# Two matmul layers after attention: five token blocks instead of six in layer 1, and two slices of h in one PSUM bank at the end of layer 2

## The chip, the cores and the metric

The kernel runs on one core of one Trainium2 chip. The time is device microseconds (us) of one execution; lower is better. TensorE (PE) multiplies, VectorE (DVE), ScalarE (ACT) and GpSimd (POOL) do the element work, SyncE (SP) issues the DMAs.

## The reference

Attention with two sparse masks (local for the first four heads, strided for the last four), then two layers over 2304 tokens, each 512 wide inside 2048 and back:

```python
x = attention(q, k, v)                       # (4*576, 512)
h = np.maximum(x @ w_in, 0.0); x1 = (h * h) @ w_out        # layer 1, w_in 512x2048, w_out 2048x512
h = x1 @ w2_in                                             # layer 2
P = a[0] + a[1]*h + a[2]*h**2 + a[3]*h**3
Q = 1.0 + abs(b[0])*abs(h) + abs(b[1])*h**2
out = (P / (Q + 1e-6)) @ w2_out
```

## The kernel before

**Numbers.** Every operand is split in a high and a low part (`xh`, `xl`; `wh`, `wl`; `gh`, `gl`), and each product is three matmuls: high by high, high by low, low by high.

**Layer 1** goes over token blocks j of `WIDTHS` columns and, in each, over 16 slices f of 128 of the 2048 inner features. `h_unit` (L414 to L420) makes one slice of h: 4 parts of the 512 inputs by 3 matmuls, 12 matmuls whose moving operand is as wide as the block, into one PSUM bank. `act1` (L426) squares and splits it on ACT, DVE and POOL. `o_unit1` (L457 to L465) adds it to four accumulators that stay in PSUM for the block: again 12 matmuls as wide as the block. It runs `LAG` = 2 slices behind. `evac1` (L467) copies the accumulators out, and they go to DRAM.

**Layer 2** goes over blocks of `WIDTHS2`. `unit2` (L664) makes h the same way, `act2` (L602) puts the rational function together (five ACT, two POOL and three DVE operations), `split2` (L633) splits the result on ACT and POOL, and `o_unit2` (L641) adds it to one accumulator per 128 tokens, with 512 columns moving. It runs `LAG2` = 4 slices behind; in blocks of 384 two slices of h come first and then two of the output. The first `EARLY` = 5 slices of layer 2 run between the last five of layer 1, here called the layer change. `load_x1` (L591) brings the next block's input from DRAM and splits it on ACT and POOL.

**Attention** is cut in pieces (`ORDER`, L232): two strided ones per batch, and one local piece per block of layer 1. The first three run ahead of layer 1. The others are spread by `PLAN` (L675): scores with softmax, transposes, and values, each at a named slice (j, f) of layer 1.

**Weights.** In block 0 those of layer 1 are converted (`feed_w`), in blocks 1 to 4 those of layer 2 (`spill_w`, L575): one load, ACT, three DVE and two POOL operations, two stores.

**Order and buffers.** A recording layer puts the instructions on each engine's queue, mostly in the order of the code, and puts in the waits. Buffers turn by tag: `g_tile` (L423) gives "r", "gh" and "gl" to both layers. PSUM has eight banks: seven turn (`psum`), and one (`psum_w`) holds converted weights in block 0 and later one accumulator or one bank of scores (`acc_bank`, L451). SP issues the DMAs in its queue's order.

Of the kernel before, what the change touches and what calls it, by code (L numbers as in the profile page):

```python
# [34 lines left out]
C_L, C_S, C_ID, C_END = 0, 384, 440, 568  # L35
# [85 lines left out]
def moe_kernel(ctx, tc, qs, vs, ql, vl, w1, w2, a, b, masks, eye, out):  # L121
# [650 lines left out]
```

## Time and profile before

| | |
|---|---|
| median of 3 runs | 863.61 us (863.11 to 866.34) |
| profiled execution: its own time, its span | 863.71 us, 861.9 us |
| busy share of the span: PE, DVE, POOL, ACT | 98%, 70%, 61%, 54% |
| layer 1, layer 2 | about 27 to 480 us, 440 to 862 us |

The span is what the profiler saw between the first and the last instruction; 1.8 us lie around it. A busy PE is one that has a matmul under way.

### The profile page before, as it was taken

Reading aid. Unit: us, or ns where it says so; the run is one execution under the profiler, and the core shown is the slowest. Engines: PE = TensorE matmul, PEld = TensorE weight load, DVE = VectorE, ACT = ScalarE, POOL = GpSimd, SP = SyncE. Lnnn points to the kernel's source line nnn. Section 1 sums busy time; section 2 is a strip of 40 time slices with the busy share of each in tenths; the row PEclk is TensorE's granted clock in tenths of the full one; section 3 lists DMA queues with packets and bytes.
Section 4 is the critical chain, followed back from the end, with each engine's and each line's share of the span. In section 5 each row is a group of like instructions: output and inputs, shape, how many; then the busy total and the mean of one; then the engine's idle time right before and its main releaser. Section 6 shows DMA issues by size and latency. Waiting matters only on the chain.

```text
span 861.9 us, 15809 instructions
## 1 busy us (share of the span) xinstructions
PE 848.7 (98%) x6141; PEld 761.3 (88%) x6146; DVE 601.7 (70%) x744; ACT 465.8 (54%) x908; POOL 529.9 (61%) x511
## 2 busy tenths in 40 slices
PE   7999999999999999999999999999999999999998
PEld 4788789999999999999998888999888889888886
DVE  6999947635556555552125788878898888889885
ACT  4555633333433334332246666776776677767663
POOL 2787736535554555563334577877787787867774
PEclk9999999999999999999999999999999999999999
DMA  9982345535554446645764400110010001000001
GB/s 339 366 285 71 105 155 185 195 96 177 155 198 155 137 135 203 203 142 172 269 234 155 144 13 13 45 38 10 9 47 12 14 13 62 1 0 37 1 1 49
DMA packets 38379, 100.04 MB, mean 116 GB/s; under 512 B 4512, under 2 KB 8352, under 8 KB 38304
## 3 DMA queue, kind: packets, MB, share of 16 engines
q1 hardware_dynamic: 38304, 99.03, 34.4%
q8 instruction: 48, 0.79, 0.4%
q14 instruction: 27, 0.22, 0.1%
HBM read 72.80 MB, written 26.21 MB: 115 GB/s over the span
## 4 chain that ended last, share of the span: by engine, by line
PE 91%; ACT 2%; DVE 2%; POOL 2%; DMA 2%; issue 1%; SPq 0%; POOLq 0%; ACTq 0%; DVEq 0%
PE h L420 44%; PE acc L650 22%; PE acc L465 21%; PE ps_vl L360 1%; DMA qkl<-in_ql 1%; DMA wraw<-in_w 1%; PE ps_vs L360 1%; PE ps_sl L299 1%; PE ps_tl L351 0%; POOL p L618 0%; PE ps_ss L299 0%; DVE h L622 0%; PE ps_ts L351 0%; DVE wraw L190 0%; POOL wl L200 0%
## 5 line engine op out<-in xcount | busy, mean ns | idle before, releaser
L420 PE MATMUL h<-xh,wh 128*128 128x384 f32 (+2 forms) x704 | 248.2, 353 | 2.2 <-DVE rq L631 1.3
L420 PE MATMUL h<-xh,wl 128*128 128x384 f32 (+2 forms) x704 | 246.4, 350 | 0.0
L420 PE MATMUL h<-xl,wh 128*128 128x384 f32 (+2 forms) x704 | 246.4, 350 | 0.0
L622 DVE RECIPROCAL h<-w 128x512 f32<-128x512 f32 (+1 forms) x80 | 242.7, 3033 | 1.0 <-POOL w L619 1.0
L618 POOL TENSOR_TENSOR p<-p,hs 128x512 f32<-128x512 f32 (+1 forms) x80 | 94.7, 1183 | 110.3 <-ACT p L616 110.3
L420 PEld LDWEIGHTS h<-xh,wh 128*128 128x128 f32 x704 | 132.4, 188 | 14.5 <-DVE rq L631 1.6
L420 PEld LDWEIGHTS h<-xl,wh 128*128 128x128 f32 x704 | 132.5, 188 | 10.5
L420 PEld LDWEIGHTS h<-xh,wl 128*128 128x128 f32 x704 | 132.3, 188 | 10.0
L465 PE MATMUL acc<-gh,wh 128*128 128x384 f32 (+2 forms) x384 | 128.8, 337 | 0.0
L465 PE MATMUL acc<-gh,wl 128*128 128x384 f32 (+2 forms) x384 | 128.6, 335 | 0.0
L465 PE MATMUL acc<-gl,wh 128*128 128x384 f32 (+2 forms) x384 | 128.6, 335 | 0.0
L443 POOL TENSOR_TENSOR gl<-r,gh 128x384 fp32r<-128x384 f32 (+1 forms) x75 | 74.4, 994 | 72.5 <-ACT gh L442 69.3
L650 PE MATMUL acc<-wh,gl 128*128 128x512 f32 x288 | 112.5, 391 | 0.4 <-POOL gl L638 0.4
L650 PE MATMUL acc<-wl,gh 128*128 128x512 f32 x288 | 112.4, 390 | 0.0
L650 PE MATMUL acc<-wh,gh 128*128 128x512 f32 x288 | 111.9, 389 | 0.0
L439 DVE TENSOR_TENSOR r<-r 128x384 f32<-128x384 f32 (+1 forms) x75 | 47.6, 634 | 88.4 <-ACT r L435 88.3
L613 ACT ACTIVATE sq<-h 128x512 f32<-128x512 f32 (+1 forms) x80 | 44.9, 561 | 115.4 <-PE h L420 111.4
L620 DVE SCALAR_TENSOR_TENSOR p<-p,co,h 128x512 f32<-128x512 f32 (+1 forms) x80 | 54.3, 679 | 67.5 <-POOL p L618 67.0
L638 POOL TENSOR_TENSOR gl<-rq,gh 128x512 fp32r<-128x512 f32 (+1 forms) x80 | 94.6, 1184 | 2.5 <-ACT gh L637 2.5
L619 POOL TENSOR_TENSOR w<-w,sq 128x512 f32<-128x512 f32 (+1 forms) x80 | 94.5, 1181 | 0.0
L435 ACT ACTIVATE r<-h 128x384 f32<-128x384 f32 (+2 forms) x91 | 44.4, 488 | 91.3 <-PE h L420 91.3
L442 ACT CAST gh<-r 128x384 fp32r<-128x384 f32 (+2 forms) x91 | 46.7, 513 | 78.7 <-DVE r L439 77.8
(109 smaller groups left out, 1339.5 us busy)
## 6 DMA issues: line engine op xcount, KB each, us to landing
wraw<-in_w SPq DMA_DIRECT2D x64, 512.0 KB, 4.3
w_scratch<-sph SPq DMA_DIRECT2D x32, 256.0 KB, 3.9
w_scratch<-spl SPq DMA_DIRECT2D x32, 256.0 KB, 3.2
wh<-w_scratch SPq DMA_DIRECT2D x16, 512.0 KB, 3.7
wl<-w_scratch SPq DMA_DIRECT2D x16, 512.0 KB, 4.6
qks<-in_qs SPq DMA_DIRECT2D x8, 585.0 KB, 5.4
out_dram<-osb SPq DMA_DIRECT2D x18, 256.0 KB, 2.1
qkl<-in_ql SPq DMA_DIRECT2D x8, 400.0 KB, 4.0
```

The lines of the kernel that those rows point to most:

```text
L420: nc.tensor.matmul(ps[:, :n], w[:, c], x, start=(kk == 0 and i == 0), stop=(kk == KT - 1 and i == 2))
L439: nc.vector.tensor_tensor(h, h, h, ALU.mult)
L442: last_act = nc.scalar.copy(gh, h).ins
L443: low = lambda: (nc.vector if psum_h or j == 0 else nc.gpsimd).tensor_tensor(gl, h, gh.bitcast(F32), ALU.subtract)
L465: nc.tensor.matmul(acc[j][e][:, : WIDTHS[j]], w[:, c], g, start=(f == 0 and i == 0), stop=(f == NF - 1 and i == 2))
L613: keep(nc.scalar.activation(sq, h, AF.Square))
L618: keep(nc.gpsimd.tensor_tensor(p1, p1, hs, ALU.mult))
L619: keep(nc.gpsimd.tensor_tensor(w, w, sq, ALU.add))
L620: keep(nc.vector.scalar_tensor_tensor(p1, p1, a1, h, ALU.add, ALU.mult))
L622: keep(nc.vector.reciprocal(h, w))
L638: keep(nc.gpsimd.tensor_tensor(gl, rq, gh.bitcast(F32), ALU.subtract))
L650: nc.tensor.matmul(p, g[:, t * P : (t + 1) * P], w[:, c], start=(f == 0 and i == 0), stop=(f == NF - 1 and i == 2))
```

## The change

Layer 1 has five blocks, of 512, 384, 512, 512 and 384 columns, where it had six (512, 256 and four of 384). So there is one local piece of attention fewer, the local pieces are up to 512 wide, and `PLAN` places the pieces in blocks 0 to 3. The layer 2 weights are converted in blocks 1 to 3 (8, 8 and 16 halves), in block 3 one in every slice. Layer 2 has four blocks of 512 and one of 256. In that last block two slices of h stand side by side in one bank, `act2` takes them together as 512 columns, and `o_unit2` adds both: 2 tiles by 2 slices by 3 matmuls. The input's places in SBUF turn in another way, the tag "r" has three buffers instead of four, the staged raw weights two instead of three. In the first five slices of layer 2 `w` and `hs` have places of their own (`whs`), and the next block's input is loaded at slices 6, 8, 10 and 12 there instead of 1, 4, 7 and 10. For the very last slice DVE adds `w` and `sq`, not POOL.

```diff
-WIDTHS = (512, 256, 384, 384, 384, 384)
+WIDTHS = (512, 384, 512, 512, 384)
-WIDTHS2 = (512, 384, 512, 384, 512)
+WIDTHS2 = (512, 512, 512, 512, 256)
+FSTEP = [512 // w for w in WIDTHS2]
-C_L, C_S, C_ID, C_END = 0, 384, 440, 568
+C_L, C_S, C_ID, C_END = 0, 576, 632, 760
...
-            raw = stage.tile([P, DM, 2], I32, tag="wraw", bufs=3, name=f"wraw{layer}_{f}_{part}")
+            raw = stage.tile([P, DM, 2], I32, tag="wraw", bufs=2, name=f"wraw{layer}_{f}_{part}")
...
-    ORDER = [("s", 0, 2), ("s", 0, 3), ("l", 0), ("l", 1), ("s", 1, 2), ("s", 1, 3), ("l", 2), ("l", 3),
-             ("s", 2, 2), ("s", 2, 3), ("l", 4), ("s", 3, 2), ("s", 3, 3), ("l", 5)]
+    ORDER = [("s", 0, 2), ("s", 0, 3), ("l", 0), ("l", 1), ("s", 1, 2), ("s", 1, 3), ("l", 2),
+             ("s", 2, 2), ("s", 2, 3), ("l", 3), ("s", 3, 2), ("s", 3, 3), ("l", 4)]
...
+        if layer and f % FSTEP[j]:
+            ps = ps[:, n:]
...
-        return gpool.tile([P, 512], dtype, tag=tag, name=name, bufs=4 if tag == "r" else 3)[:, :n]
+        return gpool.tile([P, 512], dtype, tag=tag, name=name, bufs=3)[:, :n]
...
-            acc[j] = [acc_bank(f"acc0_{j}_{e}", e == 0 and j % 2 == 1) for e in range(KT)]
+            acc[j] = [acc_bank(f"acc0_{j}_{e}", e == 0 and j in (1, 3, 4)) for e in range(KT)]
...
-        n = WIDTHS2[j]
+        n = 512
...
-        w = g_tile("gh", f"w{j}_{f}", n)
-        hs = g_tile("gl", f"hs{j}_{f}", n)
+        if j == 0 and f < EARLY:
+            pair = xpool.tile([P, 2, n], F32, tag=f"x{'hl'[f % 2]}12", name=f"whs{f}")
+            w, hs = pair[:, 0], pair[:, 1]
+        else:
+            w = g_tile("gh", f"w{j}_{f}", n)
+            hs = g_tile("gl", f"hs{j}_{f}", n)
...
-        keep(nc.gpsimd.tensor_tensor(w, w, sq, ALU.add))
+        last = (j, f) == (NB2 - 1, NF - FSTEP[-1])
+        keep((nc.vector if last else nc.gpsimd).tensor_tensor(w, w, sq, ALU.add))
...
-            for i, (g, w) in enumerate(pairs):
-                nc.tensor.matmul(p, g[:, t * P : (t + 1) * P], w[:, c], start=(f == 0 and i == 0), stop=(f == NF - 1 and i == 2))
+            for d in range(FSTEP[j]):
+                wh, wl = wt[1, f + d]
+                cg = slice(d * WIDTHS2[j] + t * P, d * WIDTHS2[j] + (t + 1) * P)
+                for i, (g, w) in enumerate(((gh, wh), (gh, wl), (gl, wh))):
+                    nc.tensor.matmul(p, g[:, cg], w[:, c], start=(f + d + i == 0), stop=(f + d == NF - 1 and i == 2))
...
-        h_unit(1, j, f, ps)
+        for d in range(FSTEP[j]):
+            h_unit(1, j, f + d, ps)
...
-        if j + 1 < NB2 and f in (1, 4, 7, 10):
-            load_x1(j + 1, f // 3)
+        if j + 1 < NB2 and f in X_AT[j > 0]:
+            load_x1(j + 1, X_AT[j > 0].index(f))
...
+    X_AT = (6, 8, 10, 12), (1, 4, 7, 10)
     PLAN = {
-        3: ((0, 2), (0, 4), (0, 5)), 4: ((0, 6), (0, 8), (0, 9)), 5: ((0, 10), (0, 12), (0, 13)), 6: ((1, 3), (1, 7), (1, 9)),
...
+        3: ((0, 2), (0, 4), (0, 5)), 4: ((0, 6), (0, 8), (0, 9)), 5: ((0, 10), (0, 12), (0, 13)), 6: ((1, 1), (1, 4), (1, 5)),
+        7: ((1, 5), (1, 8), (1, 9)), 8: ((1, 9), (1, 12), (1, 13)), 9: ((1, 13), (2, 4), (2, 5)), 10: ((2, 5), (2, 8), (2, 9)),
+        11: ((2, 9), (2, 12), (2, 13)), 12: ((2, 13), (3, 4), (3, 5)),
...
-    spills = (0, 5, 13, 21, 2 * NF)
+    spills = (0, 8, 16, 2 * NF)
...
-        if WIDTHS2[j] == 384 and f % 2 == 0:
-            continue
```

**At the layer change, POOL's queue.** Before (`p` and `w` with the slice's number are `act2`'s, `gl` is `split2`'s, `xl` is `load_x1`'s for block 1):

```order
L618 TENSOR_TENSOR p_0_5571<-p_0_5571,hs_0_5570 128x512
L619 TENSOR_TENSOR w_0_5569<-w_0_5569,sq_0_5568 128x512
L618 TENSOR_TENSOR p_1_5633<-p_1_5633,hs_1_5632 128x512
L619 TENSOR_TENSOR w_1_5631<-w_1_5631,sq_1_5630 128x512
L598 TENSOR_TENSOR xl_1_5646<-xraw_0_5647,xh_1_5645 128x384
L618 TENSOR_TENSOR p_2_5702<-p_2_5702,hs_2_5701 128x512
L619 TENSOR_TENSOR w_2_5700<-w_2_5700,sq_2_5699 128x512
L638 TENSOR_TENSOR gl_0_0_5715<-rq_0_5572,gh_0_0_5714 128x512
```

The same place of the change:

```order
L624 TENSOR_TENSOR p_0_5002<-p_0_5002,whs_5001 128x512
L626 TENSOR_TENSOR whs_5001<-whs_5001,sq_0_5000 128x512
L624 TENSOR_TENSOR p_1_5063<-p_1_5063,whs_5062 128x512
L626 TENSOR_TENSOR whs_5062<-whs_5062,sq_1_5061 128x512
L624 TENSOR_TENSOR p_2_5125<-p_2_5125,whs_5124 128x512
L626 TENSOR_TENSOR whs_5124<-whs_5124,sq_2_5123 128x512
L645 TENSOR_TENSOR gl_0_0_5138<-rq_0_5003,gh_0_0_5137 128x512
```

The split of the next block's input no longer stands between slices 1 and 2, and `w` and `hs` are parts of one `whs` tile.

**At the end of layer 2, POOL's queue.** Before, the last two slices and what follows:

```order
L618 TENSOR_TENSOR p_14_9174<-p_14_9174,hs_14_9173 128x512
L619 TENSOR_TENSOR w_14_9172<-w_14_9172,sq_14_9171 128x512
L638 TENSOR_TENSOR gl_4_12_9188<-rq_12_9087,gh_4_12_9187 128x512
L618 TENSOR_TENSOR p_15_9219<-p_15_9219,hs_15_9218 128x512
L619 TENSOR_TENSOR w_15_9217<-w_15_9217,sq_15_9216 128x512
L638 TENSOR_TENSOR gl_4_13_9231<-rq_13_9131,gh_4_13_9230 128x512
L638 TENSOR_TENSOR gl_4_14_9248<-rq_14_9175,gh_4_14_9247 128x512
L638 TENSOR_TENSOR gl_4_15_9252<-rq_15_9220,gh_4_15_9251 128x512
```

The change, where one entry is two slices:

```order
L624 TENSOR_TENSOR p_12_8435<-p_12_8435,hs_12_8434 128x512
L626 TENSOR_TENSOR w_12_8433<-w_12_8433,sq_12_8432 128x512
L645 TENSOR_TENSOR gl_4_8_8449<-rq_8_8322,gh_4_8_8448 128x512
L624 TENSOR_TENSOR p_14_8492<-p_14_8492,hs_14_8491 128x512
L645 TENSOR_TENSOR gl_4_10_8504<-rq_10_8380,gh_4_10_8503 128x512
L645 TENSOR_TENSOR gl_4_12_8521<-rq_12_8436,gh_4_12_8520 128x512
L645 TENSOR_TENSOR gl_4_14_8525<-rq_14_8493,gh_4_14_8524 128x512
```

The last `w` left this queue, so `gl` of the last slice but two (here the last entry but two) follows `p` directly.

**At the start of block 1, DVE's queue.** Before (`r` is `act1`'s square, `x` the copies of block 0's accumulators, `ps_sl` and `sm` the softmax of the local piece of block 2):

```order
L439 TENSOR_TENSOR r_1_1681<-r_1_1681 128x256
L475 COPY x_0_0_1700<-acc_0_1_728 128x512
L475 COPY x_0_2_1705<-acc_0_3_730 128x512
L439 TENSOR_TENSOR r_2_1723<-r_2_1723 128x256
L188 TENSOR_SCALAR w_1_0_0_1732<-w_1_0_0_1732 128x512
L189 SCALAR_TENSOR_TENSOR w_1_0_0_1732<-wraw_0_0_1730,w_1_0_0_1732 128x512
L190 SCALAR_TENSOR_TENSOR w_1_0_0_1732<-wraw_0_0_1730,w_1_0_0_1732 128x512
L328 TENSOR_TENSOR ps_sl_0_1759<-ps_sl_0_1759,cst 128x384
L328 TENSOR_TENSOR ps_sl_1_1760<-ps_sl_1_1760,cst 128x384
L329 TENSOR_REDUCE sm_79<-ps_sl_0_1759 128x6
```

The change:

```order
L329 TENSOR_TENSOR ps_sl_0_1702<-ps_sl_0_1702,cst 128x512
L329 TENSOR_TENSOR ps_sl_1_1703<-ps_sl_1_1703,cst 128x512
L330 TENSOR_REDUCE sm_79<-ps_sl_0_1702 128x8
L330 TENSOR_REDUCE sm_80<-ps_sl_1_1703 128x8
L339 TENSOR_TENSOR el_0_1770<-ps_sl_0_1702,sm_79 128x512
L339 TENSOR_TENSOR el_1_1779<-ps_sl_1_1703,sm_80 128x512
L442 TENSOR_TENSOR r_1_1801<-r_1_1801 128x384
L341 TENSOR_REDUCE sm_79<-el_0_1770 128x8
L341 TENSOR_REDUCE sm_80<-el_1_1779 128x8
L342 TENSOR_SCALAR sm_79<-sm_79 128x8
L477 COPY x_0_0_1820<-acc_0_1_744 128x512
```

The softmax now stands ahead of the copies that free block 0's accumulators, and works on 512 columns.

## Rows read from the trace of the kernel before

**Rows 1.** The page: busy time of the engines, and the last chain by engine.

```profile
PE 848.7 (98%) x6141; PEld 761.3 (88%) x6146; DVE 601.7 (70%) x744; ACT 465.8 (54%) x908; POOL 529.9 (61%) x511
...
PE 91%; ACT 2%; DVE 2%; POOL 2%; DMA 2%; issue 1%; SPq 0%; POOLq 0%; ACTq 0%; DVEq 0%
```

**Rows 2.** Windows: length, PE, PEld, DVE, ACT, POOL busy, clock, DMA, GB/s.

```profile
169.00:345.00 176.00, 176.00 (x1813) 173.40 (x1812) 95.34 (x193) 67.72 (x150) 89.62 (x96) 1.00 0.50 160
...
405.00:480.00 75.00, 73.11 (x396) 69.33 (x395) 26.84 (x27) 35.43 (x66) 29.90 (x26) 1.00 0.62 218
...
480.00:840.00 360.00, 360.00 (x1676) 309.09 (x1675) 307.10 (x222) 251.83 (x470) 267.18 (x235) 1.00 0.08 25
```

**Rows 3.** Timeline of PE, three widths: start us, length us, engine, line, operands.

```profile
64.28 0.39 PE L420 MATMUL h<-xh,wh 128*128 128x512 f32 x1
...
67.00 0.39 PE L465 MATMUL acc<-gh,wh 128*128 128x512 f32 x1
...
137.00 0.28 PE L420 MATMUL h<-xh,wh 128*128 128x256 f32 x1
...
138.44 0.28 PE L465 MATMUL acc<-gh,wh 128*128 128x256 f32 x1
...
237.46 0.33 PE L420 MATMUL h<-xh,wh 128*128 128x384 f32 x1
...
239.54 0.33 PE L465 MATMUL acc<-gh,wh 128*128 128x384 f32 x1
```

**Rows 4.** The last chain in order of time, a block of 384 in layer 2.

```profile
567.14 4.18 PE h L420 x24
...
571.33 4.12 PE acc L650 x18
```

**Rows 5.** PE's waits: us in total, times, longest.

```profile
PE h L420 <- DVE rq L631: 1.3, 1, 1.3
```

**Rows 6.** Timeline of ACT, POOL and PE at the layer change.

```profile
458.87 0.69 ACT L614 ACTIVATE w<-h,co 128x512 f32<-128x512 f32 x1 [1.85 <-DVE h L622]
...
465.90 1.01 POOL L598 TENSOR_TENSOR xl<-xraw,xh 128x384 fp32r<-128x384 f32 x1 [10.53 <-ACT xh L597]
...
463.97 0.44 PE L420 MATMUL h<-xh,wh 128*128 128x384 f32 x1 [0.64 <-DVE gl L443]
...
469.65 0.50 PE L420 MATMUL h<-xh,wh 128*128 128x512 f32 x1 [1.25 <-DVE rq L631]
```

**Rows 7.** Timeline of POOL and PE at the end.

```profile
847.48 1.29 POOL L619 TENSOR_TENSOR w<-w,sq 128x512 f32<-128x512 f32 x1
...
848.72 2.54 POOL L638 TENSOR_TENSOR gl<-rq,gh 128x512 fp32r<-128x512 f32 x2
...
850.07 0.50 PE L650 MATMUL acc<-wh,gl 128*128 128x512 f32 x1 [0.40 <-POOL gl L638]
```

**Rows 8.** Timeline of PE: scores of a local piece, 256 and 384 wide.

```profile
33.01 0.86 PE L299 MATMUL ps_sl<-qkl 64*32 64x64 f32 x64
...
130.05 1.17 PE L299 MATMUL ps_sl<-qkl 64*32 64x64 f32 x96
```

**Rows 9.** Groups by line and form: busy us, mean ns of one.

```profile
L622 DVE RECIPROCAL h<-w 128x512 f32<-128x512 f32 x48 | 161.0, 3354 | 1.0 <-POOL w L619 1.0
...
L620 DVE SCALAR_TENSOR_TENSOR p<-p,co,h 128x512 f32<-128x512 f32 x48 | 35.7, 745 | 46.1 <-POOL p L618 45.6
...
L631 DVE SCALAR_TENSOR_TENSOR rq<-p,co,h 128x512 f32<-128x512 f32 x48 | 35.6, 741 | 0.1
```

**Rows 10.** Timeline of ACT after the layer change.

```profile
483.80 0.60 ACT L613 ACTIVATE sq<-h 128x512 f32<-128x512 f32 x1 [3.95 <-DMA x_scratch<-x]
```

**Rows 11.** Timeline of ACT and POOL, one half of a converted weight.

```profile
375.53 0.67 ACT L187 ACTIVATE w<-wraw 128x512 f32<-128x512 f32 x1 [1.34 <-POOL spl L200]
...
379.23 1.29 POOL L200 TENSOR_TENSOR spl<-w,sph 128x512 fp32r<-128x512 f32 x1
```

**Rows 12.** Timeline of PE at the start.

```profile
4.94 0.45 PE L294 MATMUL ps_ss<-cst 128*128 128x324 bf16 x2 [0.25 <-DMA cst<-in_masks]
```

More of the change, by code (lines that the diff above doesn't have):

```diff
@@ L43, in _constants @@
     inner, first = (np.where((rel >= 0) & (rel < STRIDE), 0.0, MASKED) for rel in (q + STRIDE - k, q - k))
-    for n in range(6):
+    for n in range(9):
         for m in range(4):
-            special = (n, m) in ((0, 0), (4, 2))
+            special = (n, m) in ((0, 0), (4, 2), (7, 0))
             c[m * STRIDE : (m + 1) * STRIDE, C_L + n * EW : C_L + (n + 1) * EW] = first if special else inner
@@ L59 @@
 QS_W, QKS_W = 11 * W3, 11 * W3 + S
-QKL_W = 2 * 512
+QKL_W = 2 * 512 + STRIDE
 V_W = 2 * 6 * D
@@ L205, in x_half @@
     def x_half(layer, j, half):
-        n = j % (2, 3)[half and not layer]
+        n = ((j % 2, j % 3), (1 - j % 2, 2 * (j % 2)))[layer][half]
         if (layer, j, half) not in xt:
             xt[layer, j, half] = tuple(
-                xpool.tile([P, 2, 384 if n else 512], F32R, tag=f"x{c}{half}{n}", name=f"x{c}{half}{layer}_{j}") for c in "hl")
+                xpool.tile([P, 2, 384 if (half, n) == (1, 1) else 512], F32R, tag=f"x{c}{half}{n}", name=f"x{c}{half}{layer}_{j}") for c in "hl")
         return xt[layer, j, half]
@@ L470, in evac1 @@
             if e % 2 == 0 and j < NB - 1:
-                n = j % 2
-                pair = xpool.tile([P, 2, 384 if n else 512], F32, tag=f"x{'hl'[e // 2]}0{n}", name=f"x1_{j}_{e}")
+                pair = xpool.tile([P, 2, 512], F32, tag=f"x{'hl'[e // 2]}0{j % 2}", name=f"x1_{j}_{e}")
             t = pair[:, e % 2, :w] if j < NB - 1 else g_tile("r", f"x1_{j}_{e}", w)
@@ L644, in o_unit2 @@
         gh, gl = gt.pop((1, j, f))
-        wh, wl = wt[1, f]
         c = slice(DM, 2 * DM)
-        pairs = ((gh, wh), (gh, wl), (gl, wh))
         for t, p in enumerate(acc[1, j]):
-            for i, (g, w) in enumerate(pairs):
-                nc.tensor.matmul(p, g[:, t * P : (t + 1) * P], w[:, c], start=(f == 0 and i == 0), stop=(f == NF - 1 and i == 2))
-            if f == NF - 1:
+            for d in range(FSTEP[j]):
[3 more added lines that the diff above has]
+                    nc.tensor.matmul(p, g[:, cg], w[:, c], start=(f + d + i == 0), stop=(f + d == NF - 1 and i == 2))
+            if f + FSTEP[j] == NF:
                 last = j == NB2 - 1
-                o = g_tile("r", f"osb{j}_{t}", DM) if last else l2.tile([P, DM], F32, tag="osb", name=f"osb{j}_{t}", bufs=3)
+                if t < 2:
+                    o = xpool.tile([P, 2, 384], F32, tag=f"x{'hl'[t]}11", name=f"osb{j}_{t}").rearrange("p a b -> p (a b)")[:, :DM]
+                else:
+                    o = l2.tile([P, DM], F32, tag="osb", name=f"osb{j}_{t}", bufs=2)
                 keep((nc.vector.tensor_copy if last and t % 2 == 0 else nc.scalar.copy)(o, p))
@@ L674, in moe_kernel @@
     LAG2, EARLY = 4, 5
+    X_AT = (6, 8, 10, 12), (1, 4, 7, 10)
     PLAN = {
[3 rows of a table removed]
[3 rows of a table added]
     }
-    JOINT = {PLAN[n][2] for n in range(6, 13)}
+    JOINT = {PLAN[n][2] for n in range(6, 12)}
     def tr_both(p):
@@ L725, in moe_kernel @@
             attend((j, f))
-        elif 0 < j < 5 and f > 1 and (j, f + 1) not in JOINT and n2 < spills[j - 1] + -(-(spills[j] - spills[j - 1]) * (f + 1) // NF):
+        elif 0 < j < 4 and f > (1, 1, -1)[j - 1] and (j, f + 1) not in JOINT and n2 < spills[j - 1] + -(-(spills[j] - spills[j - 1]) * (f + 1) // NF):
             with tc.issue_after(last_act):
@@ L741, in moe_kernel @@
         finish(*prev.pop(0))
-    for j, f in [(j, f) for j in range(NB2) for f in range(NF)][EARLY:]:
+    for j, f in [(j, f) for j in range(NB2) for f in range(0, NF, FSTEP[j])][EARLY:]:
         unit2(j, f)
-        if WIDTHS2[j] == 384 and f % 2 == 0:
-            continue
         while len(prev2) > LAG2:
```

12 lines of the change are left out of this document (6 added, 6 removed), and 2 rows, old and new, of the table PLAN.

## The prediction

> **What bounds the kernel now.** I read the page first. PE is busy for 848.7 of 861.9 us and the last chain is PE for 91% [rows 1]; no other engine has more than 70%. The windows then say where PE is not saturated: in 169 to 345 us (blocks of 384 of layer 1) and in 480 to 840 us (layer 2 after the layer change) it is busy for the whole of the window, at a granted clock of 1.00, the 2.4 GHz level; only at the layer change, 405 to 480 us, are 1.89 us of idleness to be seen [rows 2]. In layer 2 DVE is busy for 307 of 360 us, so the others have some room and PE none. So an edit gains only by what it takes out of PE's own queue, or out of the few places in which PE stands: the start, the layer change and the end. It loses wherever it makes PE stand.
>
> **The change part by part.** The sum starts from the profiled execution's own 863.71 us, 0.1 above the median of 863.61.
>
> **(a) Widths of layer 1.** The timeline of PE gives the pace from the start of one group of 12 matmuls to the next. 512 wide: 67.00 - 64.28 = 2.72 us. 384 wide: 239.54 - 237.46 = 2.08. 256 wide: 138.44 - 137.00 = 1.44 [rows 3]. A slice of layer 1 is two such groups. Before: 16 x (5.44 + 2.88 + 4 x 4.16) = 399.36 us. After, three blocks of 512 and two of 384: 16 x (3 x 5.44 + 2 x 4.16) = 394.24. That is **-5.12 us**. The three paces lie on a line, 0.64 us for 128 columns in 12 matmuls, or 53.3 ns each, and a matmul of no columns would then cost 2.08/12 - 3 x 0.0533 = 0.0133 us. Each block takes 16 x 24 = 384 matmuls, so one block fewer saves 384 x 13.3 ns = 5.1 us: the columns are the same, the fixed part is paid less often. In layer 2 there are five blocks and 18 tiles of 128 tokens before and after, so the matmuls and the columns are equal there. The bound of this term is the timeline's two decimals: 0.01 us a group, 192 groups fewer or wider, below 1 us.
>
> The Trainium skill (TensorE: Matmul & The Clock Gate, section "Wait — 56ns, not 53.3ns?") states a fixed part of some 2.5 ns on top of columns over the clock. By it this term would be, as an estimate, 384 x 2.5 ns, about 1 us, which speaks against most of the gain. The paces of this trace give 13.3 ns with float32 operands, and I go by them.
>
> **(b) One local piece of attention fewer.** The scores of a 256-wide piece take 0.86 us and of a 384-wide one 1.17 [rows 8]: 0.31 for 32 matmuls more, so the fixed part is 0.86 - 0.62 = 0.24. The query blocks are the same in number, so only fixed parts go: about **-0.2** (0 to -0.7, three such switches for scores, transposes and values).
>
> **(c) The layer change.** Before, PE waits there for DVE's `rq` and for a `gl`, [1.25] and [0.64] before two matmuls of h [rows 6]; the first is the 1.3 of the list of waits [rows 5]. Three rows say why. ACT's `w` waits 1.85 us for a reciprocal, since it takes a "gh" buffer that an earlier slice holds. POOL's `xl` stands 10.53 us for its `xh`, and `p` and `w` of slice 2 are queued behind it. Then PE's h needs a bank that DVE frees late. After, `whs` has places that no one else needs at that time, and `xl` is not between slices 1 and 2 in POOL's queue (first place shown above). The wait for `rq` (1.25) and for `gl` (0.64) then go: 1.89 us, the same that the window has [rows 2]. The ends of matmuls are modelled, so a little more than the idle time shown is lost around a stop; I add 0.15 for each by choice: **-2.2** (0 if another wait takes their place, -2.4 if twice as much is added). What is late next is not PE by the rows: a slice there asks 3354 + 745 + 741 ns of DVE = 4.84 us [rows 9] for its layer 2 part, and a joint slice (layer 1 at 384 and layer 2 at 512) is some 4.16 + 2.72 = 6.9 us of PE; 2.0 us are left to DVE for its part in layer 1.
>
> **(d) The end.** POOL begins the last `w` at 847.48, then does two `gl` in a row from 848.72; PE waits [0.40] for the first of them and its matmul begins at 850.07 [rows 7]. In that order `w` is ahead of `gl`: 1.29 us that `gl` need not stand behind. After, DVE adds `w` (second place above), as `gl` goes straight behind `p`. What it gives lies between the 0.40 shown and the whole 1.29; since PE's ends are modelled, I take a value near the middle, **-0.75** (-0.3 if `gl` of the last entry is late instead, -0.85 as the favourable bound, for the last entry's own chain allows no more). For that entry: from the end of the last h to the last o are four steps of o, 10.9 us both before and after, and DVE's addition, at most some 0.75 us (L620's 745 ns, of the same size [rows 9]), takes the place of POOL's 1.29 in its chain, but stands behind the `rq` of the entry ahead.
>
> **(e) Changes of shape in layer 2.** In blocks of 384 two slices of h take 4.18 us and two of the output 4.12 [rows 4], 8.30 in all, where paces give 24 x 2.08/12 + 18 x 2.72/12 = 4.16 + 4.08 = 8.24. So 0.06 a pair, 16 pairs, 1.0 us. After, only the last block mixes 256 with 512, in 8 entries: I leave 0.3 us. **-0.7** (0 to -1.1).
>
> **(f) The start.** The table of masks `cst` grows by a third (columns 568 to 760) and PE waits [0.25] for it [rows 12]; a third of that is about 0.1. Block 0's local piece stays 512. **+0.1** (0 to +1).
>
> What costs nothing, with its cover. Three "r" buffers: after the change `sq` of slice 5 waits for block 1's input, as ACT does now, [3.95] at 483.80 [rows 10], without a stop of PE; at LAG2 = 4 slices a result has 4 x 5.44 = 21.8 us before PE needs it, and the chain from h to `gl` is three times 1.29 on POOL [rows 7], 4.84 on DVE [rows 9] and six of 0.60 to 0.69 on ACT [rows 6, 10], some 12.6 in all, were nothing side by side. Conversion of layer 2 weights in every slice of block 3: one half now goes from ACT's piece at 375.53 to POOL's last at 379.23 + 1.29 = 380.5, 5.0 us [rows 11], against a slice of 5.44. Local pieces of 512 instead of 384: a third more work for DVE and ACT in each, but fewer pieces.
>
> Sum: 863.71 - 5.12 - 0.2 - 2.2 - 0.75 - 0.7 + 0.1 = 854.84. I say **855.0 us**. With every bound at its unfavourable end (0 for b, c and e, -0.3 for d, +1 for f, 4.1 for a) it is 860.3; at its favourable one 863.71 - 6.1 - 0.7 - 2.4 - 0.85 - 1.1 = 852.6.
>
> **The rivals.**
>
> A. The layer change gives nothing: a new wait takes the place of the old. For it: "r" has three buffers, and ACT's `sq` then stands behind the DMA that brings x_scratch (3.95 now [rows 10]), while DVE holds the banks of h until the reciprocal. Against it: the 9 us and more by which results are early there (21.8 less 12.6, above). Price: 2.2 us, 854.8 + 2.2 = **857.0**.
>
> B. Block 1 makes PE stand. There the softmax is now ahead of the copies that free block 0's accumulators, and works on 512 columns instead of 384 (third place above). Until the copies are done four of the eight banks are held, two more hold scores, and the h slices share what is left. For it: the largest stops of PE now, 1.3 to 1.5 us, are of the sort "waits for DVE". Against it: PE is busy for all of 169 to 345 us though pieces of 384 were worked in there too [rows 2], and the seven operations of 512 or less ahead of the copies take at most 0.75 us each [rows 9], 5.3 us, against the two slices, 8.3 us, by which o runs behind h; 3 us are left. Price: one stop of 1.3 us [rows 5] at each of the three joint slices of scores and values in block 1, 3.9 us: **858.8**.
>
> C, on the other side: conversion in block 3 is the bound. Each of its 16 slices has one half to convert, through one chain ACT, DVE, POOL, DVE, POOL with two staged raw buffers. Where a half takes longer than a slice of 5.44 us, the chain falls behind by the excess each time, and DVE's and ACT's layer 1 work in the same queues with it; LAG hides some 7.6 us of it: two slices of 5.44, less a chain of five operations of 0.6 to 0.75 in layer 1 [rows 9, 10], 3.3 us, an estimate. Now it takes 5.0, and ACT's own row there shows that it stands 1.34 us for POOL's `spl` [rows 11]. It decides from (16 x excess - 7.6) > 8.9 us, an excess of 1.03: a half of 6.5 us. With 7 us it is 16 x 1.56 - 7.6 = 17.4 us of stops, 854.8 + 17.4 = **872**. Against it: no half in the trace takes that long, and a slice of 512 gives each engine a third more time than one of 384.
>
> D. The change doesn't do what it says: the 13.3 ns are not paid by each matmul, but are time in which PE stands for operands, and the wider blocks pay it too. Then only b to f are left: 863.71 - 3.75 = **860.0**. Against it: block 0 shows the 512-wide pace already, and three widths lie on one line [rows 3]. The rule on the fixed part that the Trainium skill states (page and section as in a) would lead to nearly the same, an estimate of 859.
>
> **How the numbers follow.** Forecast as worked out, 853.6 to 856.9: 0.62. A: 0.11. B, or several small stops of its size: 0.13. C: 0.05. D: 0.03. Better than 853.6: 0.06. A measurement of this kernel can tell about 0.5% from no change, that is 859.3 on the faster side and 867.9 on the slower. Faster: the forecast, A, the better case, and B but for its dearer part, 0.62 + 0.11 + 0.06 + 0.09 = 0.88. The same: 0.04 of B, D, and 0.01 of C, 0.08. Slower: 0.04. The range that leaves some 2 in 10 out goes from 853.4 (a part of the better case) to 859.0 (A and most of B).
>
> **What the profile after would show.** (a) groups of 12 with a pace of 2.72 and 2.08 us in every block, and layer 1 shorter by 5 us. (c) no wait of PE for `rq` at the layer change and no `xl` with a wait of 10 us between its slices. (d) no wait of PE for POOL's `gl` at the end. (e) all of layer 2 in steps of 5.44 us, and entries of 5.6 to 5.7 in the last block. Rival A would show as PE waiting for `rq`, `gl` or the reciprocal around slice 5 of layer 2, B as waits of h for DVE's copies `x` or of transposes for `el` in block 1, C as waits of o for `gl` late in block 3 with spans of more than 5.44 us between `spl`. Most likely to make me wrong are stops in block 1, since DVE's and PSUM's turn there is new and no row of before shows it.

## The result and the profile after

The changed kernel takes 855.45 us (median of 6 executions, 854.41 to 861.02) against 864.01 for the kernel before in the same measurement (6 executions, 863.11 to 866.34). The ratio is 0.9911, with a 95% interval of 0.9882 to 0.9939 (the ratios are worked out from the executions and are not the quotients of the medians). The forecast was 855.0, range 853.4 to 859.0.

The profiled execution took 857.55 us, 2.1 more than the median. Its page: busy time by engine, and the last chain.

```profile
PE 846.5 (99%) x5762; PEld 720.0 (84%) x5762; DVE 600.3 (70%) x688; ACT 453.6 (53%) x821; POOL 523.2 (61%) x468
...
PE 98%; DVE 1%; DMA 0%; ACT 0%; issue 0%; POOL 0%; SPq 0%; ACTq 0%; POOLq 0%
```

The chain is PE for 98% where it was 91% [rows 1]. Windows answer to those of before [rows 2]: length; busy time of PE, PEld, DVE, ACT, POOL; granted clock; DMA share; GB/s.

```profile
140.00:300.00 160.00, 160.00 (x1589) 142.72 (x1588) 90.49 (x170) 58.17 (x120) 76.96 (x80) 1.00 0.45 145
300.00:386.00 86.00, 86.00 (x473) 71.20 (x472) 46.76 (x65) 31.18 (x53) 51.67 (x46) 1.00 0.61 196
402.00:475.00 73.00, 73.00 (x398) 69.90 (x397) 28.14 (x27) 34.49 (x65) 29.56 (x25) 1.00 0.67 233
475.00:840.00 365.00, 365.00 (x1702) 306.13 (x1701) 309.58 (x201) 250.34 (x432) 268.75 (x214) 1.00 0.08 25
```

PE stands nowhere in them, the layer change (402 to 475) included. The list of PE's waits is complete here, and every wait in it lies in the first 28 us: no `rq`, no `gl` is left of those that stood there before [rows 5 to 7].

```profile
PE ps_ts L352 <- POOL eas L344: 1.9, 2, 1.4
PE ps_ss L490 <- DVE warm L485: 1.5, 1, 1.5
PE ps_vs L361 <- ACT eas L354: 1.0, 1, 1.0
PE ps_vl L361 <- ACT eal L354: 0.5, 1, 0.5
PE ps_vs L361 <- issue: 0.5, 1, 0.5
PE ps_ss L295 <- DMA cst<-in_masks: 0.2, 1, 0.2
```

To find the gain I cut both executions at three instructions on PE: the first h of layer 1, the first output of layer 2 (both kernels have done the same work by then but for widths and the one piece of attention), and the last matmul. Timeline of PE, before:

```profile
27.11 0.47 PE L420 MATMUL h<-xh,wh 128*128 128x512 f32 x1
...
479.46 0.39 PE L650 MATMUL acc<-wh,gh 128*128 128x512 f32 x1
...
857.70 0.39 PE L650 MATMUL acc<-wh,gl 128*128 128x512 f32 x1
```

And of the changed kernel:

```profile
30.21 0.47 PE L423 MATMUL h<-xh,wh 128*128 128x512 f32 x1
...
474.84 0.39 PE L658 MATMUL acc<-wh,gh 128*128 128x512 f32 x1
...
851.69 0.39 PE L658 MATMUL acc<-wh,gl 128*128 128x512 f32 x1
```

Call the time from the first to the second cut stretch 1, and from the second to 0.23 us after the start of the last matmul (its pace) stretch 2. Beside each stands what its matmuls of layers 1 and 2 would take at the paces of [rows 3]; the difference is attention, stops and changes of shape.

| kernel | first h | stretch 1 | at pace | over | stretch 2 | at pace | over |
|---|---|---|---|---|---|---|---|
| before | 27.11 | 452.35 | 415.68 | 36.67 | 378.47 | 376.64 | 1.83 |
| changed | 30.21 | 444.63 | 410.56 | 34.07 | 377.08 | 376.64 | 0.44 |
| changed minus before | +3.10 | -7.72 | -5.12 | -2.60 | -1.39 | 0 | -1.39 |

Terms a, b and c of the prediction belong to stretch 1 and were forecast at -7.52; d and e belong to stretch 2 and were forecast at -1.45. Only the start is off: +3.10 in this execution, where +0.1 was forecast. The windows of PE alone (length, busy, granted clock, DMA share, GB/s) show why:

```profile
0.00:12.00 12.00, 8.90 (x120) 1.00 0.86 319
12.00:16.00 4.00, 3.58 (x93) 0.61 0.99 362
16.00:28.00 12.00, 9.93 (x220) 0.84 0.98 350
```

At 0.61 and 0.84 part of the time is at the lower level, 1.2 GHz. The profiled execution of before has 1.00 in all three windows. PE stands for POOL's `eas` for 1.4 us just ahead of the fall, but it stands for that in the execution of before too. So this +3.10 is not a size of the change: three other runs with the changed start, at a clock of 1.00 up to there, have their first h at 26.93 to 27.10 (layer 1 alone, both parts of the layer change undone, old loads with own copies).

### The profile page after: what moved, and what is told of

Same layout as the page of the kernel before. It is cut to its first block, busy times and chain, and to the rows that moved or that the text cites. A ratio compares the mean times of both kernels' runs of the same rounds, so it can differ in the third digit from the quotient of the medians.

```text
span 855.8 us, 14872 instructions
## 1 busy us (share of the span) xinstructions
PE 846.5 (99%) x5762; PEld 720.0 (84%) x5762; DVE 600.3 (70%) x688; ACT 453.6 (53%) x821; POOL 523.2 (61%) x468
## 4 chain that ended last, share of the span: by engine, by line
PE 98%; DVE 1%; DMA 0%; ACT 0%; issue 0%; POOL 0%; SPq 0%; ACTq 0%; POOLq 0%
PE h L423 46%; PE acc L468 23%; PE acc L658 23%; PE ps_vl L361 1%; PE ps_sl L300 1%; PE ps_vs L361 1%; PE ps_ss L300 1%; PE ps_tl L352 1%; PE ps_ts L352 1%; DMA cst<-in_masks 0%; DVE sm L330 0%; PE ps_tl L490 0%; DVE sm L341 0%; PE ps_ss L295 0%; PE ps_sl L295 0%; DVE eal L339 0%
## 5 line engine op out<-in xcount | busy, mean ns | idle before, releaser
L423 PE MATMUL h<-xh,wh 128*128 128x512 f32 (+2 forms) x640 | 237.0, 371 | 0.0
L423 PE MATMUL h<-xh,wl 128*128 128x512 f32 (+2 forms) x640 | 235.6, 368 | 0.0
L423 PE MATMUL h<-xl,wh 128*128 128x512 f32 (+2 forms) x640 | 235.6, 368 | 0.0
L629 DVE RECIPROCAL h<-w 128x512 f32<-128x512 f32 x67 | 224.6, 3353 | 0.0
L624 POOL TENSOR_TENSOR p<-p,hs 128x512 f32<-128x512 f32 x67 | 86.9, 1297 | 97.6 <-ACT p L622 97.5
L468 PE MATMUL acc<-gh,wh 128*128 128x512 f32 (+1 forms) x320 | 118.2, 369 | 0.0
L468 PE MATMUL acc<-gh,wl 128*128 128x512 f32 (+1 forms) x320 | 117.7, 368 | 0.0
L468 PE MATMUL acc<-gl,wh 128*128 128x512 f32 (+1 forms) x320 | 117.6, 367 | 0.0
L645 POOL TENSOR_TENSOR gl<-rq,gh 128x512 fp32r<-128x512 f32 x72 | 93.4, 1298 | 3.2 <-ACT gh L644 3.2
L626 POOL TENSOR_TENSOR w<-w,sq 128x512 f32<-128x512 f32 x66 | 85.5, 1296 | 0.0
```

The lines of the kernel that those rows point to most:

```text
L423: nc.tensor.matmul(ps[:, :n], w[:, c], x, start=(kk == 0 and i == 0), stop=(kk == KT - 1 and i == 2))
L468: nc.tensor.matmul(acc[j][e][:, : WIDTHS[j]], w[:, c], g, start=(f == 0 and i == 0), stop=(f == NF - 1 and i == 2))
L624: keep(nc.gpsimd.tensor_tensor(p1, p1, hs, ALU.mult))
L626: keep((nc.vector if last else nc.gpsimd).tensor_tensor(w, w, sq, ALU.add))
L629: keep(nc.vector.reciprocal(h, w))
L645: keep(nc.gpsimd.tensor_tensor(gl, rq, gh.bitcast(F32), ALU.subtract))
```

## The experiments

Times are medians with the kernel before on the same chip beside them; stretches are those of the table above, from each run's own trace. All runs are the changed kernel with the edit shown, unless another is named.

**Layer 1 alone.**

```diff
-WIDTHS2 = (512, 512, 512, 512, 256)
+WIDTHS2 = (512, 384, 512, 384, 512)
...
-        if j == 0 and f < EARLY:
+        if False:
...
-    X_AT = (6, 8, 10, 12), (1, 4, 7, 10)
+    X_AT = (1, 4, 7, 10), (1, 4, 7, 10)
...
-        keep((nc.vector if last else nc.gpsimd).tensor_tensor(w, w, sq, ALU.add))
+        keep(nc.gpsimd.tensor_tensor(w, w, sq, ALU.add))
```

(and, with these widths, one slice of h in a bank and two slices at a time in blocks of 384, as before)

> The changed kernel with layer 2 as it was before: blocks of 512, 384, 512, 384, 512, places of w and hs, times of the input's loads and the last sum on POOL as before. Layer 1's five blocks, attention's places and the larger table of masks stay. Theory (each matmul has a fixed part of 13.3 ns and there are 384 fewer): from layer 1's first h to layer 2's first output the trace is 5.1 to 5.5 us shorter than before's 452.35, and the rest after it is as before, 378.5; the time is 863.7 - 5.1 - 0.2 + 0.6 (later start) = 859.0. Rival 1 (the fixed part is some 2.5 ns, by the Trainium skill, TensorE: Matmul & The Clock Gate, Wait - 56ns, not 53.3ns?): that stretch is about 1 us shorter, and the time 863.3. Rival 2 (the change gains by layer 2 and the layer change alone): 864.2.

859.58 us against 864.22, ratio 0.9925 (0.9885 to 0.9965). First h 27.10, at a granted clock of 1.00. Timeline of PE, the two ends of stretch 1:

```profile
27.10 0.47 PE L423 MATMUL h<-xh,wh 128*128 128x512 f32 x1
...
474.13 0.39 PE L658 MATMUL acc<-wh,gh 128*128 128x512 f32 x1
```

Stretch 1 is 447.03: 5.32 shorter than before, of which 5.12 is the widths at pace. The 0.20 left over is the size of term b, but it does not show term b: the profiled execution of before has one short stop in this stretch that the second trace with the old layer 1 (before with the larger table, below) does not have.

```profile
95.76 0.50 PE L420 MATMUL h<-xh,wh 128*128 128x512 f32 x1 [0.32 <-ACT r L435]
```

In that second trace stretch 1 is 452.10, so 5.07 is gained, the widths alone. Rival 1 and rival 2 fall. Stretch 2 is 379.23, 0.76 longer than before: ACT's `sq` now waits 7.98 us where it waited 3.95 [rows 10], and a wait of PE for POOL's `gl` has come up behind it. Timeline of ACT and PE:

```profile
482.50 0.60 ACT L619 ACTIVATE sq<-h 128x512 f32<-128x512 f32 x1 [7.98 <-DMA x_scratch<-x]
...
488.76 0.50 PE L658 MATMUL acc<-wh,gl 128*128 128x512 f32 x1 [0.37 <-POOL gl L645]
```

This is rival A's wait, and it is there as soon as layer 1 is changed; the runs on the layer change show where it comes from.

**The pace by itself.** A kernel that leaves the whole computation out.

```diff
+    run("warm", 512, WARM, True)
+    for n in (512, 384, 256, 128):
+        run(f"many{n}", n, N, True)
+    for n in (512, 384):
+        ps = run(f"one{n}", n, N, False)
+    last = run("one256", 256, N, False)
```

(`WARM` is 60 and `N` is 96 matmuls; `True` takes eight pieces of weights in turn, `False` one piece)

> A kernel that leaves the whole computation out: 60 matmuls of 512 columns, then 96 each of 512, 384, 256 and 128 columns with eight pieces of weights in turn, then 96 each of 512, 384 and 256 with one piece of weights, all float32 in the form that the kernel uses; the output is filled with the last sums. Theory (13.3 ns fixed in each matmul and 53.3 ns for 128 columns): 226.7, 173.3, 120.0 and 66.7 ns a matmul at a granted clock of 1.00, the same with one piece of weights. Rival 1 (the fixed part comes from the change of weights): with one piece it is 213.3, 160.0 and 106.7. Rival 2 (below some width the load of weights sets the pace): 128 columns well above 66.7, near the 100 ns and more that a load takes in the traces.

Groups by form, PE and then its weight loads: busy us, mean ns of one, idle time before.

```profile
L34 PE MATMUL one<-m,w 128*128 128x512 f32 x96 | 22.0, 390 | 0.0
L34 PE MATMUL many<-m,w 128*128 128x512 f32 x96 | 21.9, 389 | 0.0
L34 PE MATMUL many<-m,w 128*128 128x384 f32 x96 | 16.8, 334 | 0.0
...
L34 PE MATMUL many<-m,w 128*128 128x256 f32 x96 | 11.7, 283 | 0.0
...
L34 PE MATMUL many<-m,w 128*128 128x128 f32 x96 | 10.8, 274 | 0.0
...
L34 PEld LDWEIGHTS many<-m,w 128*128 128x128 f32 x384 | 57.1, 190 | 3.8
L34 PEld LDWEIGHTS one<-m,w 128*128 128x128 f32 x288 | 46.3, 189 | 3.8
```

All of them ran at a granted clock of 1.00. A busy time holds 95 paces and one whole matmul, so the pace is (21.9 - 0.389)/95 = 226.4 ns for 512 columns, 173.3 for 384, 120.2 for 256: the forecast to 0.4 ns, and no wait of the kernel is in it. For 128 columns it is 110.8, not 66.7: the line ends between 256 and 128 columns, as rival 2 said. That the load of weights sets that pace is argued only; a load takes 190 ns and lies beside the matmul ahead. Rival 1 could not be told: the kernel with one piece of weights loads it 288 times for 288 matmuls all the same. So that each matmul pays the 13.3 ns is shown, and what in it costs them is not.

**Widths of layer 2 undone** (first edit of the first diff alone, with the slices as in its parenthesis).

> The changed kernel with layer 2 in blocks of 512, 384, 512, 384, 512 again, one slice of h in a bank; all else as changed. Theory (every change between 384 and 512 costs some 0.06 us a pair of slices, 16 pairs): from layer 2's first output to the last matmul 1.0 to 1.1 us above the pace of 376.64, so 377.7, against 377.08 in the changed kernel and 378.47 before; the time rises by 0.6. Rival (changes of shape cost nothing, and all of the 1.4 us gained there came from the last sum on DVE): no difference, 377.1.

856.22 us against 864.22, ratio 0.9891 (0.983 to 0.9951). Stretch 2 is 378.15, 1.07 longer than the changed kernel's 377.08, with no wait of PE in it. The rival falls. The theory's direction holds and its size does not: 1.51 above the pace, where 1.0 to 1.1 was expected. Stretch 1 is not read: this execution's first h came at 34.01, and stretch 1 began at a granted clock of 0.50.

**Last sum on POOL** (last edit of the first diff alone).

> The changed kernel with the last slices' w added on POOL again. Theory (gl of the last entry but two stands behind w in POOL's queue): PE waits 0.4 us or more for POOL's gl at the end again, and from layer 2's first output to the last matmul 0.7 to 0.8 us more than 377.08; the time rises by 0.75. Rival (with two slices in an entry POOL has done w before gl's operand is there): no wait, no difference.

856.78 us against 864.44, ratio 0.9915 (0.9894 to 0.9936). POOL at the end, and PE's one wait there:

```profile
840.78 1.29 POOL L624 TENSOR_TENSOR p<-p,hs 128x512 f32<-128x512 f32 x1 [1.81 <-ACT p L622]
842.03 1.29 POOL L626 TENSOR_TENSOR w<-w,sq 128x512 f32<-128x512 f32 x1
843.27 2.54 POOL L645 TENSOR_TENSOR gl<-rq,gh 128x512 fp32r<-128x512 f32 x2
...
844.62 0.50 PE L658 MATMUL acc<-wh,gl 128*128 128x512 f32 x1 [0.43 <-POOL gl L645]
```

`gl` follows `w` again and PE's wait is back, so the rival falls. Stretch 2 is 377.52, so this edit is worth 0.44 us, the idle time and hardly more; 0.7 to 0.8 was expected.

**The layer change: both parts undone, and each alone** (second and third edit of the first diff together, the second alone, the third alone).

> The changed kernel with w and hs of the first five slices of layer 2 in the turning buffers again, and the input of block 1 loaded at slices 1, 4, 7 and 10 again. Theory: PE waits at the layer change again, for rq and for gl, 1.9 us idle, and from layer 1's first h to layer 2's first output 2.2 us more than the changed kernel's 444.63; the time rises by 2.2. Rival (with the new widths the waits do not come back, and the 2.6 us gained there came from attention and the widths): no idle time of PE, within 0.3 of 444.63.

> The changed kernel with only the places of w and hs undone, the later loads kept. Theory: the 1.25 us wait of PE for rq comes back, since ACT's w waits for a buffer that layer 1 holds, and the 0.64 for gl does not; some 1.4 us more than 444.63 from layer 1's first h to layer 2's first output. Rival (only the loads made the waits): no idle time of PE, no difference.

> The changed kernel with only the loads of block 1's input back at slices 1, 4, 7 and 10 of the first block of layer 2, the places of w and hs kept. Theory: POOL's xl waits some 10 us between slices 1 and 2 for a place that layer 1 reads to its end, p and w of slice 2 are behind it, and PE waits 0.6 to 1.3 us for a bank or a result. Rival (results are early enough for POOL to be late by that): POOL waits, PE does not, no difference in 444.63.

| kernel | time, before | ratio | stretch 1 | stretch 2 | PE waits in them |
|---|---|---|---|---|---|
| changed | 855.45, 864.01 | 0.9911 | 444.63 | 377.08 | none |
| both undone | 858.99, 864.22 | 0.9939 (0.990 to 0.9977) | 447.82 | 377.90 | `xl` 0.23, `gl` 0.63, `rq` 1.47, `gl` 0.44 |
| own places undone | 860.53, 864.44 | 0.9955 (0.9936 to 0.9973) | 449.20 | 377.08 | `rq` 0.26, `gl` 2.19 |
| old loads | 862.87, 864.44 | 0.9981 (0.9968 to 0.9994) | 446.49 | 381.52 | `rq` 1.48, `gh` 0.34, `gl` 1.89 |

With both undone the two waits of [rows 6] come back at the same places, 3.2 us in stretch 1 and 0.8 in stretch 2; 2.2 was expected. About 0.5 of the 3.2 belongs to the start: the first h is early there (26.93), PE then waits 0.23 for `xl`, and by the fourth matmul of h it has lost 0.48 against layer 1 alone. Either part undone alone costs more than both, which none of the expectations had. With the own places alone undone that surplus comes with the clock: PE stands 2.45 us there and 2.54 with both undone, but the granted clock falls after the long stop (last section), and the one execution of it at 1.00 as a whole took 856.99 us, where the fastest with both undone, also at 1.00, took 857.61. With the old loads alone PE stands longer, 3.71 us, and the clock falls besides. Two chains lead to the stops.

Own places undone: timeline of ACT and PE.

```profile
448.37 0.69 ACT L620 ACTIVATE w<-h,co 128x512 f32<-128x512 f32 x1 [0.84 <-DVE h L629]
...
464.29 0.69 ACT L620 ACTIVATE w<-h,co 128x512 f32<-128x512 f32 x1 [2.87 <-DVE h L629]
...
472.26 0.69 ACT L620 ACTIVATE w<-h,co 128x512 f32<-128x512 f32 x1 [3.02 <-DVE h L629]
...
472.73 0.44 PE L468 MATMUL acc<-gl,wh 128*128 128x384 f32 x1 [2.19 <-DVE gl L446]
```

Each `w` starts only when the reciprocal of the slice ahead has ended; in the changed kernel, with places of its own, it waits for nothing. The wait grows from slice to slice, 0.84, 1.85, 2.87 and 3.02 us, since the loop ACT `w`, POOL, DVE reciprocal goes round in 7.97 us (464.29 to 472.26) and PE's joint slice takes 6.95. At the end layer 1's last `gl` is late by that on DVE, and PE stands 2.19. The expectation had the right cause, but the wait in the wrong place: `rq` came back with 0.26 only, and the long stop is for `gl`.

Old loads: ACT and PE after the layer change.

```profile
485.49 0.60 ACT L619 ACTIVATE sq<-h 128x512 f32<-128x512 f32 x1 [10.17 <-DMA x_scratch<-x]
...
489.08 0.50 PE L658 MATMUL acc<-wh,gh 128*128 128x512 f32 x1 [0.34 <-ACT gh L644]
491.71 0.50 PE L658 MATMUL acc<-wh,gl 128*128 128x512 f32 x1 [1.89 <-POOL gl L645]
```

POOL's `xl` waits 10.70 us there, as it did before [rows 6], DVE is late by it, so are the copies of block 4's accumulators and their stores; and `sq` needs one of the three "r" buffers that these copies hold. In the changed kernel the same instruction waits too, at 479.72, and PE does not stop:

```profile
479.72 0.60 ACT L619 ACTIVATE sq<-h 128x512 f32<-128x512 f32 x1 [6.17 <-DMA x_scratch<-x]
```

**Old loads, with the copies in places of their own** (beside the third edit of the first diff).

```diff
-            t = pair[:, e % 2, :w] if j < NB - 1 else g_tile("r", f"x1_{j}_{e}", w)
+            elif e % 2 == 0:
+                pair = xpool.tile([P, 2, 384], F32, tag=f"x{'hl'[e // 2]}11", name=f"x1_{j}_{e}")
+            t = pair[:, e % 2, :w]
```

> The changed kernel with the old loads, as in the run with the old loads alone, but block 4's copies of the accumulators go to places that no one else needs then, not to the three r buffers. Theory (rival A's wait: sq stands behind the stores of these copies, 10.17 us in that run, and so PE waits 1.89 us for gl after the layer change): ACT's sq no longer waits for x_scratch, PE's waits of 0.34 and 1.89 us for gh and gl vanish, and the stretch from layer 2's first output is 377.1 to 377.6 instead of 381.5; the 1.48 us for rq stays. Rival (POOL's queue alone makes gl late): the waits stay, 381.

856.88 us against 864.04, ratio 0.9926 (0.9907 to 0.9944). Stretch 1 is 446.51 with the wait of 1.5 for `rq`, stretch 2 is 377.12 with none, and `sq` no longer waits for the DMA. So the 4.4 us that the old loads cost in stretch 2 came through the three "r" buffers: it is shown by taking away that claim alone. Of these 4.4, 2.23 are PE's idle time, and some 1.3 of the rest are the lower clock behind it (5 or 6 matmuls of 0.23 us, last section). The other 1.9 in stretch 1 stay with the old loads; that they come from POOL's queue, in which `xl` stands 10.70 us here too, fits the trace, and no run takes it apart.

**The table of masks.** Two runs: before with the larger table (`C_S, C_ID, C_END = 576, 632, 760`), and the changed kernel with the table in two loads.

```diff
-    load(cst, masks)
+    load(cst, masks[:, C_S:])
...
     load(ident, eye)
+    load(cstl, masks[:, :C_S])
```

(and every read of the table goes to its part)

> The kernel before with only its table of masks as large as in the changed kernel (760 columns instead of 568, 190 KB instead of 142); nothing else changes. Theory (the later start of the changed kernel comes from this table, which stands ahead of the second piece's input in SP's queue): PE's first score 0.3 us later than 5.32 or more, layer 1's first h 0.5 to 0.7 us later than 27.11 where the granted clock stays at 1.00, and up to 3 us later where it falls to the lower level in the first 28 us. Rival (the later start comes from the larger input of the second local piece, loaded at 23 us): layer 1's first h within 0.2 us of 27.11.

> The changed kernel with the table of masks in two loads: the part of the strided pieces and the identity (184 columns, 46 KB) first, the part of the local pieces (576 columns) after the identity of the transposes. Theory (the first scores wait for the table's bytes): PE's first score at 5.0 to 5.2 us instead of 5.90, layer 1's first h 0.6 to 0.9 us earlier than in the changed kernel at the same granted clock, so some 26.6 where the clock stays at 1.00; the time 854.0 to 854.6 against 855.0. Rival (the first scores wait for their own input, and the table's size does not matter): no difference.

Before with the larger table: 864.0 us against 864.22, ratio 0.9987 (0.9961 to 1.0013). Timeline of PE:

```profile
5.82 0.37 PE L299 MATMUL ps_ss<-qks 64*64 64x54 f32 x4
...
27.14 0.47 PE L420 MATMUL h<-xh,wh 128*128 128x512 f32 x1
```

The first score is 0.50 us later than before (5.32), the first h 0.03: something later than the table sets the first h, and the rival holds. In two loads: 856.35 against 864.44, ratio 0.9907 (0.9892 to 0.9922), first score 5.62, first h 27.62 at a clock of 1.00, where 5.0 to 5.2 and 26.6 were expected: no gain. The theory, that the table makes the start later, falls; the table's own price, term f, is 0.03 us.

**The start: the same kernel again, and more fill.**

```diff
-'t00': 6, 't01': 2, 's2': 2, 't10': 2, 'v1': 4, 't20': 4, 't21': 2, 'h0': 3}
+'t00': 10, 't01': 3, 's2': 2, 't10': 2, 'v1': 8, 't20': 5, 't21': 2, 'v2': 2, 'h0': 3}
```

> The changed kernel once more, unaltered, for the spread of its start. Theory (the 3.1 us that its profiled execution lost at the start are the granted clock of that execution alone): executions from 854.4 to 861, most near 855; in an execution at a granted clock of 1.00 layer 1's first h begins at 27.0 to 27.6, and the two stretches after it are 444.6 and 377.1 again. Rival (the changed kernel's start is later by itself): first h at 30 in every execution, at any clock.

> The changed kernel with more of the idle-time matmuls (fill) ahead of transposes and values of the first three pieces: 10 instead of 6, 3 instead of 2, 8 instead of 4, 5 instead of 4, and 2 where there were none; they compute nothing that is used. Theory (the granted clock falls in some executions after PE has stood for 1.0 to 1.5 us at a time in the first 27 us): PE's waits of 1.45 and 1.0 us shrink to 0.6 or less, the clock stays at 1.00 in more executions, and the median falls by 0.5 to 1.5 us below that of the changed kernel in the same call. Rival (the fall has nothing to do with these waits): the same share of executions falls, and the median is the same or up to 0.5 us higher by the longer queue.

The changed kernel again: 855.48 us against 864.04, ratio 0.9899 (0.9884 to 0.9914), executions of 854.69 to 856.46. Its first h is at 27.87, the two stretches are 444.67 and 377.09. So what the program does after its start is the same to 0.04 us, and 2.3 of the 3.1 us at the start were that one execution's. The 0.76 that is left was not free of the clock either. Window of PE in this execution:

```profile
16.00:28.00 12.00, 9.98 (x202) 0.86 0.98 347
```

So this run does not show the start at a clock of 1.00 that its theory asks for; the three runs named with the result do. With more fill the granted clock was 1.00 in all four executions, where it had been 0.998 or 0.999 in the four of the changed kernel; PE's waits for `eas` shrank to 0.8 us in all (from 1.5). The median is 855.86, so the gain of 0.5 to 1.5 us that was expected did not come: first h at 27.72, and stretch 1 at 445.30, with a new wait of 0.4 for POOL's `wh` in it. The clock held in these four executions, and what that may have given was lost again to the longer queue: at the same clock the shorter one reaches its first h at 27.1. Four executions against four do not prove that the fill holds the clock.

## Why the prediction was right

The time lay 0.45 us from the forecast. The mechanism of a, c, d and e was shown; b is too small to be seen, and f had it wrong. That the total came out so close is in part luck: terms a to e were forecast at -8.97 and the two stretches gained 9.11, while the medians moved by 8.56 only. So about half a us is lost outside the stretches in a usual execution, at the start by the trace of the second one (+0.76 at a granted clock of 0.86), and no term had the clock in it. Forecast and measured:

| term | forecast | measured | by |
|---|---|---|---|
| a, widths of layer 1 | -5.12 | -5.07 to -5.32, with b | layer 1 alone, against the two traces with the old layer 1 |
| b, one piece fewer | -0.2 | not seen, within 0.2 of nothing | what a's -5.12 leaves |
| c, layer change | -2.2 | -2.40 | 447.03 (layer 1 alone) to 444.63 |
| d, last sum | -0.75 | -0.44 | last sum on POOL |
| e, changes of shape | -0.7 | -1.07 | widths of layer 2 undone |
| f, start | +0.1 | +0.03 by the table; +0.8 and +3.1 with a lower clock | the table alone; the two traces of the changed kernel |

- **a.** The fixed part is 13.3 ns in the kernel and in the matmuls alone. The Trainium skill's 2.5 ns (TensorE: Matmul & The Clock Gate, "Wait — 56ns, not 53.3ns?") would have left, as an estimate, 4 us of the gain out; for these float32 operands this trace disagrees. Rival D is out.
- **c** had the right waits, but its two causes are not two terms that add. The runs apart also say which wait hangs on which: the long one for `rq` (1.48) on the loads, that for `gl` (2.19) on the places of `w` and `hs`. The wait of `sq` for the copies in the "r" buffers, which costs 0.8 us in stretch 2 with layer 1 alone, goes with it as well, and the forecast had no term for that.
- **d and e** were both mis-sized, by +0.31 and -0.37, and their errors cancel: -1.45 forecast, -1.39 in stretch 2 (-1.51 by the two runs apart). In d the time that I added to the idle 0.40 was not there. In e the last block has changes of shape too, but PE takes 5.62 us an entry there, where the pace gives 2.88 + 2.72 = 5.60, so the 0.3 that I left for its 8 entries was too much; the rest of the miss lies in the 0.06 a pair, which was too little. One entry of the changed kernel, from the last chain:

```profile
795.96 2.87 PE h L423 x24
798.84 2.75 PE acc L658 x12
```

- **f** took a third of PE's 0.25 us wait as the price of the table. The step that failed is that a later first score makes a later first h: 0.50 later at the score was 0.03 at the h.
- **Rival A** did not come about, but it was near: `sq` waits 6.17 us where it had waited 3.95 [rows 10] and PE goes on; at 7.98 and 8.08 (layer 1 alone, both parts undone) PE stops for 0.37 and 0.44, and at 10.17 for 1.89. So the cover was not the "9 us and more" of the prediction but, as an estimate from 7.98 - 0.37, some 7.6. **Rival B**: no wait of PE lies in block 1; of the four largest stops before, which the prediction put down to DVE, 1.49 and 1.25 are for DVE and 1.45 and 1.44 for ACT and POOL. **Rival C**: POOL's 16 `spl` in block 3 come 5.71 us apart in the mean, most of them by about 5.44, and four gaps are 6.2 to 6.8. PE's slices there are 5.44 too, and the two with attention in them longer; the `LAG` of two slices is left to cover the rest, and PE does not wait. Timeline of POOL, the two longest gaps and a usual one:

```profile
328.25 1.29 POOL L201 TENSOR_TENSOR spl<-w,sph 128x512 fp32r<-128x512 f32 x1
...
335.05 1.29 POOL L201 TENSOR_TENSOR spl<-w,sph 128x512 fp32r<-128x512 f32 x1
...
341.89 1.29 POOL L201 TENSOR_TENSOR spl<-w,sph 128x512 fp32r<-128x512 f32 x1
...
347.33 1.29 POOL L201 TENSOR_TENSOR spl<-w,sph 128x512 fp32r<-128x512 f32 x1
```

Left open: which instruction sets the first h at 27.1, what in a matmul the 13.3 ns are, and whether the changed start meets the lower clock more often than the old one. Of the nine traces with the changed start six show a granted clock below 1.00 between 12 and 28 us, of the two with the old start none. Two are too few, and executions of the kernel before without a trace go down to a granted clock of 0.994 as a whole.

## What to carry to other kernels

Where one engine is busy throughout, count its instructions and their pace by shape: the same columns in fewer, wider instructions gained the fixed part here and nothing else that could be seen, and the rest of the sum is the few places where the engine stands. Cut the trace at three or four instructions that both kernels have, and compare stretch by stretch with the pace: two traces of the changed kernel agree to 0.04 us so, where whole executions differ by 2. Take two traces of the kernel before as well: a single short stop in one of its executions, 0.32 us, was as large as the smallest term. Edits that free a queue and a buffer at the same place should be tried apart as well as together, since one alone can be worse than neither, as the old loads alone were.

## What the runs showed of the hardware

In two traces a stop of PE of some 2 us was followed by a lower granted clock; the stops of 1.25 to 1.5 us at the layer change, in six traces, were not. No run varies the length of the stop alone. Windows of PE in the run with the old loads, around its waits of 0.34 and 1.89 us:

```profile
470.00:488.00 18.00, 18.00 (x83) 1.00 0.55 176
488.00:492.00 4.00, 1.77 (x7) 1.00 0.00 0
492.00:496.00 4.00, 4.00 (x12) 0.57 0.01 2
496.00:500.00 4.00, 4.00 (x19) 1.00 0.00 0
```

The 2.23 us of waiting became 4.44 us of stretch 2: in the 4 us at 0.57 PE did 12 matmuls, where 17 or 18 fit at pace. In the run without own places, whose stop of 2.19 ended at 472.73:

```profile
475.00:480.00 5.00, 5.00 (x20) 0.76 0.60 192
```

A matmul of 128 columns came at 110.8 ns, hardly less than one of 256 columns at 120.2.
